# A fused attention and two-MLP kernel: another written order for its attention steps, and another split of the softmax sums

## The chip, the core and the metric

The kernel runs on one core of one Trainium2 chip. The metric is device time in microseconds (us), from start to end of one execution; a kernel's time is the median of three runs. The engines are TensorE (PE; its loads of weights are listed apart, as PEld), VectorE (DVE), ScalarE (ACT), GpSimd (POOL) and the queue that issues the transfers, SyncE (SP). Each engine works off its own list of instructions in order and waits on semaphores for what others have to deliver.

## What is computed

Attention in which two neighbouring queries are averaged first, and then two MLPs, all in 32-bit floats:

```python
# q, k, v: (2, 8, 1152, 64); q and k are scaled by 8 after the draw
q_pool = q.reshape(B, H, S // 2, 2, D).mean(axis=3)
scores = np.matmul(q_pool, k.transpose(0, 1, 3, 2)) / np.sqrt(D)
scores = scores - np.max(scores, axis=-1, keepdims=True)
attn = np.exp(scores)
attn = attn / (np.sum(attn, axis=-1, keepdims=True) + 1e-09)
x = np.matmul(attn, v)            # -> 1152 tokens x 512
h = x @ w_in                      # 512 x 2048
x = (h * np.tanh(softplus(h))) @ w_out          # 2048 x 512
h = x @ w_in2
out = np.where(h > 0, h, np.exp(np.minimum(h, 0)) - 1) @ w_out2
```

The MLP weights arrive as 64-bit floats and are turned into 32-bit floats on the chip, from their two 32-bit words.

## The kernel before

The program has two parts, `attention()` and then `mlps()`, and it orders everything itself: no scheduler moves an instruction.

**Attention** goes over eight pairs of heads (pairs 0 to 7, two heads side by side in the 128 partitions). A pair has 576 averaged queries, cut into a front part of 256 (c = 0) and a back part of 320 (c = 1), and nine tiles of 128 keys. The steps of a pair, with the two letters that the written order uses for them and the line that shows in the profile:

- LK, LQ, LV load keys, queries and values. PQ (L245) adds the two queries of a couple, HQ/DQ (L250, L253) and HK/DK/DF/HD (L265, L268, L274, L282, L278) split queries and keys into a high part and a small remainder for TensorE. In pair 0 the same steps come in pieces: XP, XH, XL, XK, XM.
- PM (L308, L315, L322, L325) multiplies high parts only, to find a bound of each row's largest score; PK (L332 to L337) reduces these products on VectorE; TP (L346, L349) takes the maximum over the pieces, TO and TI carry it through DRAM into a row `top` (in pair 0 FL and FC turn it on TensorE and ScalarE, L356 and L363).
- QK (L406, and L413 for the row `top`) makes the scores of one key tile (in the front part of two tiles at once), three products for the accuracy of 32 bits. EX (L424) takes the exponential into `pt`, which exists once for each part.
- AV (L498) multiplies the nine tiles of `pt` with the values.
- The sum over the keys, the divisor of the softmax, is made in SU (L452): TensorE multiplies with a matrix of ones and so adds over the 128 partitions. What it is fed is set by the table `SUMS`, one word of nine digits for each pair and part: a tile with 0 is multiplied directly; the tiles with 1 are first added to one another in a chain, AD (L436), on VectorE or GpSimd as the step's last digit says (1 or 0); the neighbouring tiles with 2 are added by one VectorE instruction, the gather GA (L441). So a word like 111111111 costs TensorE one product (four instructions of 32 columns of ones, which the profile lists as eight) and eight adds elsewhere; every 0 costs one more product, a chain that runs along with 2s gives two.
- SP, SO, SI, IN (L477), IO, II bring the sums through DRAM to their reciprocals and spread them; EV (L510) empties the AV product from its bank; SC (L515) scales it; TH and TL (L518, L522) split the result into XH and XL, the input of the MLPs.
- W steps prepare the first four weight slices of the MLP (WR loads, WB, WC on GpSimd, L126; WS, WW on VectorE, L131, L136, L137; WH, WL, L149).

All of PM, QK, AV and FL share four pairs of PSUM banks; the digit behind the tile number is the pair of banks. TensorE cannot begin a step before the reader of the former one on these banks (PK, EX, EV with SP) is through, and it does nothing else in the meantime.

The sequence of all these steps is the written list `ORDER`, 927 steps that the loop at the end of `attention()` calls one after the other; each step appends its instructions to the lists of its engines. `REST` holds steps of pair 7 that are put into the first units of the MLPs.

**The MLPs** go over 96 units (48 a layer) of 384 tokens by 128 hidden columns, the products L182 and L727. They are written by a loop of their own.

## Time and profile before

| | us |
|---|---|
| median of three runs (616.83 to 618.44) | 617.96 |
| the profiled execution's own time | 617.06 |
| its span, first to last instruction | 615.3 |
| TensorE busy | 595.5 (97%) |
| VectorE busy | 468.3 (76%) |
| ScalarE busy | 346.0 (56%) |
| GpSimd busy | 200.6 (33%) |

The span ends some 2 us short of the execution's own time. A matmul counts as busy from its issue to its modelled end, so a row of matmuls that come slowly still looks busy. The attention steps fill the first 213.19 us; there the engines lie much closer together than in these sums.

### The profile page before, as it was taken

Reading aid. Unit: us, or ns where it says so; the run is one execution under the profiler, and the core shown is the slowest. Engines: PE = TensorE matmul, PEld = TensorE weight load, DVE = VectorE, ACT = ScalarE, POOL = GpSimd, SP = SyncE. Lnnn points to the kernel's source line nnn. Section 1 sums busy time; section 2 is a strip of 40 time slices with the busy share of each in tenths; the row PEclk is TensorE's granted clock in tenths of the full one; section 3 lists DMA queues with packets and bytes.
Section 4 is the critical chain, followed back from the end, with each engine's and each line's share of the span. In section 5 each row is a group of like instructions: output and inputs, shape, how many; then the busy total and the mean of one; then the engine's idle time right before and its main releaser. Section 6 shows DMA issues by size and latency. Waiting matters only on the chain.

```text
span 615.3 us, 12110 instructions
## 1 busy us (share of the span) xinstructions
PE 595.5 (97%) x4856; PEld 517.7 (84%) x4856; DVE 468.3 (76%) x704; ACT 346.0 (56%) x666; POOL 200.6 (33%) x190
## 2 busy tenths in 40 slices
PE   5799999999999999999999999999999999999997
PEld 4576676676676699999999999999999999999996
DVE  6999999898995676754756667669878788995453
ACT  3677577675665555443454453466657667664442
POOL 5859567695482511111132323232110101100000
PEclk9989999999999999999999999999999999999999
DMA  8434255242221024322214222222132223300011
GB/s 281 147 97 143 64 156 162 54 128 76 74 50 22 13 80 148 118 64 92 94 45 137 69 69 80 92 70 73 66 102 70 68 69 107 122 13 17 36 52 51
DMA packets 46962, 53.39 MB, mean 87 GB/s; under 512 B 13818, under 2 KB 36410, under 8 KB 46906
## 3 DMA queue, kind: packets, MB, share of 16 engines
q1 hardware_dynamic: 46618, 52.22, 27.4%
q8 instruction: 38, 0.62, 0.5%
q10 hardware_dynamic: 288, 0.39, 0.2%
q14 instruction: 18, 0.15, 0.1%
HBM read 50.14 MB, written 2.47 MB: 85 GB/s over the span
## 4 chain that ended last, share of the span: by engine, by line
PE 82%; DVE 10%; DMA 2%; issue 2%; ACT 2%; POOL 1%; SPq 0%; POOLq 0%; DVEq 0%
PE banks L182 33%; PE banks L727 32%; PE banks L498 8%; PE banks L406 5%; DVE stat L332 4%; ACT pt L424 1%; PE banks L308 1%; PE banks L452 1%; DVE add L436 1%; POOL add L436 1%; DVE wf L137 1%; DMA top<-hopm 1%; DMA kr<-in_k_dram 1%; DMA tot<-hop 1%; PE banks L413 1%
## 5 line engine op out<-in xcount | busy, mean ns | idle before, releaser
L182 PE MATMUL banks<-XH,wl 128*128 128x384 f32 x384 | 128.4, 334 | 0.0
L182 PE MATMUL banks<-XL,wh 128*128 128x384 f32 x384 | 128.4, 334 | 0.0
L182 PE MATMUL banks<-XH,wh 128*128 128x384 f32 x384 | 128.3, 334 | 0.0
L126 POOL TENSOR_SCALAR wf<-wf 128x512 f32<-128x512 f32 x64 | 42.9, 671 | 257.1 <-ACT wf L122 226.9
L424 ACT ACTIVATE pt<-banks 128x640 f32<-128x640 f32 (+2 forms) x112 | 84.1, 790 | 23.5 <-PE banks L406 15.2
L332 DVE TENSOR_REDUCE stat<-banks 128x2 f32<-128x1024 f32 (+1 forms) x68 | 76.4, 1168 | 4.0 <-PE banks L308 3.5
L498 PE MATMUL banks<-pt,vr 128*32 128x320 f32 (+1 forms) x1152 | 73.2, 407 | 0.7 <-DVE stat L334 0.5
L182 PEld LDWEIGHTS banks<-XH,wh 128*128 128x128 f32 x384 | 72.1, 188 | 2.0 <-issue 0.3
L182 PEld LDWEIGHTS banks<-XL,wh 128*128 128x128 f32 x384 | 72.1, 188 | 1.6
L182 PEld LDWEIGHTS banks<-XH,wl 128*128 128x128 f32 x384 | 72.1, 188 | 0.0
L679 ACT ACTIVATE gh<-banks 128x384 fp32r<-128x384 f32 x48 | 23.7, 493 | 72.0 <-PE banks L182 72.0
L727 PE MATMUL banks<-gh,wh 128*128 128x384 f32 x192 | 64.1, 334 | 0.0
L727 PE MATMUL banks<-gl,wh 128*128 128x384 f32 x192 | 64.1, 334 | 0.0
L727 PE MATMUL banks<-gh,wl 128*128 128x384 f32 x192 | 64.1, 334 | 0.0
L498 PEld LDWEIGHTS banks<-pt,vr 128*32 128x32 f32 x1152 | 35.8, 110 | 33.3 <-ACT pt L424 1.9
L436 POOL TENSOR_TENSOR add<-add,pt 128x512 f32<-128x512 f32 (+1 forms) x35 | 51.6, 1475 | 27.2 <-DVE add L436 10.5
L727 PE MATMUL banks<-wl,gh 128*128 128x512 f32 x144 | 56.3, 391 | 0.0
L727 PE MATMUL banks<-wh,gl 128*128 128x512 f32 x144 | 56.2, 390 | 0.0
L727 PE MATMUL banks<-wh,gh 128*128 128x512 f32 x144 | 56.1, 390 | 0.0
L682 DVE TENSOR_TENSOR gl<-g,gh 128x384 fp32r<-128x384 f32 x48 | 32.5, 676 | 30.7 <-ACT g L680 30.6
L706 ACT CAST gh<-g 128x384 fp32r<-128x384 f32 x48 | 24.7, 515 | 48.1 <-DVE g L700 47.8
L137 DVE SCALAR_TENSOR_TENSOR wf<-raw,wf 128x512 int32<-128x512 int32 x64 | 48.0, 751 | 2.2
(101 smaller groups left out, 1219.7 us busy)
## 6 DMA issues: line engine op xcount, KB each, us to landing
raw<-in_moe_w_in_dram SPq DMA_DIRECT2D x28, 512.0 KB
raw<-in_moe_w_out_dram SPq DMA_DIRECT2D x28, 512.0 KB
vr<-in_v_dram SPq DMA_DIRECT2D x16, 288.0 KB
qr<-in_q_dram SPq DMA_DIRECT2D x14, 288.0 KB
kr<-in_k_dram SPq DMA_DIRECT2D x7, 384.0 KB
out_dram<-part SPq DMA_DIRECT2D x9, 256.0 KB
raw<-in_moe_w_in_dram SPq DMA_DIRECT2D x8, 256.0 KB
raw<-in_moe_w_out_dram SPq DMA_DIRECT2D x8, 256.0 KB
```

The costliest lines, as they stand in the source:

```text
L126: eng.tensor_scalar(self.f, self.f, HUGE, -HUGE, op0=ALU.min, op1=ALU.max)
L137: nc.vector.scalar_tensor_tensor(f, self.low, 29, f, op0=ALU.logical_shift_right, op1=ALU.bitwise_or)
L182: nc.tensor.matmul(pt[:, :TB], w[:, kk * P:(kk + 1) * P], x[:, kk, tk], start=(i == 0), stop=(i == len(terms) - 1))
L332: nc.vector.tensor_reduce(m[:, t, :, j], pt[:, :, :kw], axis=AX.X, op=ALU.max)
L406: nc.tensor.matmul(pt[:, h, t * w:(t + 1) * w], x[half[h], k0 + t * P:k0 + (t + 1) * P], y[half[h], cols], start=(z == t == 0 and not on), ...
L424: nc.scalar.activation(pts[n, c][:, kt:kt + m], pt, AF.Exp, scale=SCALE)
L436: eng.tensor_tensor(d, p[:, ch[0]] if len(ch) == 2 else d, p[:, k], op=ALU.add)
L498: nc.tensor.matmul(acc[n, c][32 * g:32 * (g + 1), 0, :w], vs[n][:, h, kt, 32 * z:32 * (z + 1)], pts[n, c][:, kt, h, :], start=(kt == 0), s ...
L679: nc.scalar.activation(gh, h, AF.Mish)
L682: nc.vector.tensor_tensor(gl, g, gh, op=ALU.subtract)
L706: nc.scalar.copy(gh, g)
L727: nc.tensor.matmul(pt, l, r, start=(first and i == 0), stop=(final and i == 2))
```

## The change

The list `ORDER` is written anew (920 steps), and so are `SUMS` and `REST`. Every step is the same code as before. No function changes. The word of digits of a pair's part, before and now (pair 0 to 7, front and back):

```diff
             SUMS = """
-            110122010 101111122 011111220 000022101 221111110 000111221 221111111 100111111
-            222111101 011111111 101111100 111111111 221111110 111111111 111111111 111111111
+            000002220 101101222 100001222 001011101 111110101 111100222 221111111 111102211
+            110111110 111110222 110111110 111101222 111101111 111111222 111111111 111111111
             """.split()
             ORDER = """
-            LV00 XP01 LV01 XK0 XH0 WR00 PM003 XM00 WR01 XK1 WR10 XP11 PM012 XM10 XK2 PK00 WR11 XH1 LV11 PM040 PK01
+            LV00 XP01 WR00 XK0 XH0 WR01 PM002 LV10 XK1 LV11 PK00 XP10 PM010 WR10 XM00 XH1 XK2 WR11 PM023 PK01 XL00
...
             REST = [
-                "SP70 SP71 SO70 SO71 SI70",
-                "SI71 IN70 IO70",
-                "IN71 IO71 II70",
-                "II71 SC70 TH70 TL70",
-                "SC71 TH71 TL71",
+                "IO70 EV71 SP71 II70",
+                "SO71",
+                "SI71 SC70 TH70",
+                "IN71 IO71 II71",
+                "SC71 TL70 TH71 TL71",
             ]
```

Counted over the attention: 48 products of sums become 52. The adds on VectorE go from 39 to 26, those on GpSimd from 47 to 50. The nine gathers stay nine: of two tiles of the front part 5 become 1, of three tiles of the front part 1 becomes 2, of two tiles of the back part 3 become none, of three tiles of the back part none become 6. Some splits and poolings change their engine.

Three places show how instructions move. The first is the list of TensorE around the front part of pair 0: the AV products (L498), the sums' products (L452; `pt` is a direct tile, `add` a chain or a gather), and the first peak products of pair 1. Before:

```order
L308 MATMUL banks<-KH,QH 128x384 x2
L325 MATMUL banks<-KH,blk_88 128x384 x3
L498 MATMUL banks<-pt,vr 32x256 x36
L452 MATMUL banks<-pt,ones 32x128 x12
L452 MATMUL banks<-add,ones 32x128 x8
L308 MATMUL banks<-KH,QH 128x512 x6
```

And now:

```order
L325 MATMUL banks<-KH,blk_88 128x384 x3
L406 MATMUL banks<-QH,KH 128x256 x2
L406 MATMUL banks<-QH,KL 128x256 x2
L406 MATMUL banks<-QL,KH 128x256 x2
L413 MATMUL banks<-top_84,unit 128x256 x2
L308 MATMUL banks<-KH,QH 128x384 x6
L498 MATMUL banks<-pt,vr 32x256 x36
L452 MATMUL banks<-pt,ones 32x128 x24
L452 MATMUL banks<-add,ones 32x128 x4
L308 MATMUL banks<-KH,QH 128x512 x6
```

Six tiles go directly into the product instead of three, the chain is gone and one gather is left; the other peak products of pair 0 now stand together ahead of AV.

The second is VectorE's list at the first peaks of pair 1 (L332 of 512 columns, L334, L336), with the weight steps (L131, L136, L137) and the first reciprocal (L477). Before:

```order
L441 TENSOR_REDUCE add<-pt 128x512
L131 TENSOR_SCALAR wf<-wf 128x512
L136 SCALAR_TENSOR_TENSOR wf<-raw,wf 128x512
L137 SCALAR_TENSOR_TENSOR wf<-raw,wf 128x512
L332 TENSOR_REDUCE stat<-banks 128x2 x2
L334 TENSOR_REDUCE stat<-banks 128x2x4
L332 TENSOR_REDUCE stat<-banks 128x2
L477 RECIPROCAL tot<-tot 128x4
L332 TENSOR_REDUCE stat<-banks 128x2
L346 TENSOR_REDUCE neg<-stat 128x2x2
```

And now, with the gather (L441) further up, ahead of two peaks and the maximum of pair 0:

```order
L441 TENSOR_REDUCE add<-pt 128x512
L332 TENSOR_REDUCE stat<-banks 128x2 x2
L346 TENSOR_REDUCE pad<-stat 128x4
L349 TENSOR_REDUCE pad<-stat 128x2
L131 TENSOR_SCALAR wf<-wf 128x512
L136 SCALAR_TENSOR_TENSOR wf<-raw,wf 128x512
L137 SCALAR_TENSOR_TENSOR wf<-raw,wf 128x512
L332 TENSOR_REDUCE stat<-banks 128x2 x3
L334 TENSOR_REDUCE stat<-banks 128x2x4
L336 TENSOR_REDUCE stat<-banks 128x2
L337 TENSOR_REDUCE stat<-banks 128x1
L332 TENSOR_REDUCE stat<-banks 128x2
```

The reciprocal, which stood between two peaks, now comes five rows behind these, after the maximum of pair 1 and another weight.

The third is VectorE's list between the back AV product of pair 5 and the front one of pair 6. Before:

```order
L274 TENSOR_TENSOR dr<-kr 128x896
L268 TENSOR_TENSOR KL<-kr,KH 128x256
L477 RECIPROCAL tot<-tot 128x4
L436 TENSOR_TENSOR add<-add,pt 128x640
L441 TENSOR_REDUCE add<-pt 128x512
L522 TENSOR_TENSOR XL<-out,XH 128x320
L332 TENSOR_REDUCE stat<-banks 128x2 x7
L436 TENSOR_TENSOR add<-add,pt 128x640
L334 TENSOR_REDUCE stat<-banks 128x2x4
```

And now:

```order
L274 TENSOR_TENSOR dr<-kr 128x896
L441 TENSOR_REDUCE add<-pt 128x640
L515 TENSOR_TENSOR out<-out,rb 128x320
L522 TENSOR_TENSOR XL<-out,XH 128x320
L477 RECIPROCAL tot<-tot 128x4
L332 TENSOR_REDUCE stat<-banks 128x2 x7
L477 RECIPROCAL tot<-tot 128x5
L334 TENSOR_REDUCE stat<-banks 128x2x4
```

The two adds of the back part are gone from here; a gather of three tiles of pair 5's back part takes the place of a gather of two tiles of pair 6's front part.

## Rows read from the trace of the kernel before

**Rows 1.** Busy time by stretch: us, then busy (count) of each engine, clock, DMA

```profile
0.00:69.45 69.45, 56.90 (x668) 41.66 (x668) 61.75 (x72) 41.56 (x76) 48.59 (x51) 0.95 0.49 153
69.45:166.86 97.41, 94.78 (x1375) 65.31 (x1373) 89.40 (x117) 65.04 (x109) 64.87 (x46) 1.00 0.38 109
166.86:182.25 15.39, 14.98 (x195) 10.64 (x193) 15.34 (x20) 12.03 (x19) 10.57 (x7) 1.00 0.25 49
182.25:213.19 30.94, 30.51 (x466) 19.49 (x466) 20.54 (x34) 15.40 (x27) 12.13 (x8) 1.00 0.09 18
213.19:615.30 402.11, 398.31 (x2164) 380.63 (x2160) 281.28 (x464) 212.01 (x440) 64.42 (x80) 1.00 0.24 77
```

**Rows 2.** TensorE in order of time (start, length): AV, sums' products, first MLP product

```profile
69.45 5.05 PE L498 MATMUL banks<-pt,vr 128*32 128x320 f32 x72
74.32 1.54 PE L452 MATMUL banks<-pt,ones 128*32 128x160 f32 x40
...
166.86 5.05 PE L498 MATMUL banks<-pt,vr 128*32 128x320 f32 x72
...
182.25 4.09 PE L498 MATMUL banks<-pt,vr 128*32 128x256 f32 x72
...
213.19 0.44 PE L182 MATMUL banks<-XH,wh 128*128 128x384 f32 x1
```

**Rows 3.** VectorE in the attention by line and form: busy, mean ns, idle before

```profile
L436 DVE TENSOR_TENSOR add<-add,pt 128x640 f32<-128x640 f32 x25 | 25.1, 1005 | 4.6 <-POOL add L436 4.2 <-ACT pt L424 0.2
L436 DVE TENSOR_TENSOR add<-add,pt 128x512 f32<-128x512 f32 x10 | 8.0, 803 | 3.2 <-ACT pt L424 3.1
L441 DVE TENSOR_REDUCE add<-pt 128x512 f32<-128x1024 f32 x5 | 6.2, 1245 | 0.0
L282 DVE TENSOR_TENSOR KL<-dr,DH 128x896 fp32r<-128x896 f32 x4 | 4.7, 1186 | 0.2 <-ACT DH L278 0.2
L441 DVE TENSOR_REDUCE add<-pt 128x640 f32<-128x1280 f32 x3 | 4.5, 1515 | 0.0
L441 DVE TENSOR_REDUCE add<-pt 128x512 f32<-128x1536 f32 x1 | 1.9, 1918 | 0.0
L274 DVE TENSOR_TENSOR dr<-kr 128x896 f32<-128x896 f32 x1 | 1.1, 1084 | 0.0
L253 DVE TENSOR_TENSOR QL<-qr,QH 128x576 fp32r<-128x576 f32 x1 | 0.8, 752 | 0.0
```

**Rows 4.** VectorE in order of time: instructions that waited or were held up

```profile
5.11 1.00 DVE L245 TENSOR_TENSOR qr<-qr 128x128 f32<-128x128 f32 x1 [1.02 <-DMA qr<-in_q_dram]
...
25.80 2.47 DVE L137 SCALAR_TENSOR_TENSOR wf<-raw,wf 128x512 int32<-128x512 int32 x1
...
33.59 0.18 DVE L477 RECIPROCAL tot<-tot 128x4 f32<-128x4 f32 x1 [0.79 <-DMA tot<-hop]
...
42.58 2.74 DVE L436 TENSOR_TENSOR add<-add,pt 128x640 f32<-128x640 f32 x1
...
172.66 8.01 DVE L332 TENSOR_REDUCE stat<-banks 128x2 f32<-128x1024 f32 x7
```

**Rows 5.** GpSimd in order of time, at two of these

```profile
25.18 2.55 POOL L282 TENSOR_TENSOR KL<-dr,DH 128x896 fp32r<-128x896 f32 x1
...
42.33 2.31 POOL L274 TENSOR_TENSOR dr<-kr 128x896 f32<-128x896 f32 x1
```

**Rows 6.** GpSimd by line and form

```profile
L436 POOL TENSOR_TENSOR add<-add,pt 128x512 f32<-128x512 f32 x22 | 29.9, 1358 | 11.8 <-DVE tot L477 6.8 <-DVE add L436 2.4 <-ACT pt L424 1.7
L436 POOL TENSOR_TENSOR add<-add,pt 128x640 f32<-128x640 f32 x13 | 21.7, 1673 | 15.4 <-DVE add L436 8.1 <-DVE neg L346 4.4 <-ACT pt L424 2.8
L274 POOL TENSOR_TENSOR dr<-kr 128x896 f32<-128x896 f32 x6 | 12.9, 2150 | 0.0
```

**Rows 7.** Busy time in two short stretches (columns as in the first group)

```profile
28.00:32.00 4.00, 1.76 (x11) 1.12 (x12) 4.00 (x5) 1.28 (x2) 3.21 (x3) 0.76 0.64 166
32.00:36.00 4.00, 4.00 (x21) 3.57 (x23) 3.18 (x6) 0.94 (x4) 1.12 (x2) 0.50 0.43 137
```

More of the change, by code (lines that the diff above doesn't have):

```diff
@@ new lines, in attention @@
+            PK18 QK0120 PQ20 EX012 PK13 QK0152 QK0113 EX015 TP10 WS2 QK0170 TO10 EX011 WW2 QK0141 EX017 QK0162 EX014
+            IN00 QK0183 AD0150 AD0121 EX016 TI10 PM190 QK0131 EX018 IO00 PK19 QK0102 WR40 EX013 PM163 EX010 PM171
+            AD0130 PK16 QK1000 HK21 HQ2 II00 PK17 HK20 PM152 AD0100 AV01309 EX100 PK15 DK200 TP11 GA01 DF20 TO11 WR50
+            WR51 TI11 SC00 TH00 SU01 WH2 TL00 LV20 EV01 WL21 LV21 PM251 SP01 HD2 QK1020 SO01 PK25 LK30 PM232 BQ2 PM213
+            DK210 LK31 EX102 PK23 WR41 QK1101 WB3 QK1040 PK21 EX110 PM222 WC3 EX104 QK1121 DQ20 PK22 QK1113 EX112
@@ new lines, in attention @@
+            II40 PM650 EX508 QK5143 TP60 PK65 QK5111 AD5040 TO60 EX514 LK70 PM692 EX511 QK5163 PK69 AD5050 PM670 EX516
+            QK5131 PK67 EX513 PM662 QK5183 AD5070 TI60 QK5151 IN41 SC40 AV50009 IO41 AD5060 TH40 EX518 TL40 EX515
+            AD5101 AD5120 PK66 II41 AD5151 AD5110 SU50 EV50 PM6830 SP50 SO50 QK5171 PK68 AD5130 QK6002 HK70 SI50 HQ7
+            TP61 AV51007 DF71 TO61 DK700 EX517 HK71 GA51 HD7 TI61 DQ70 SC41 AV51079 TH41 EX600 TL41 IN50 SU51 IO50
+            EV51 AD6000 AD6010 PM713 SP51 QK6022 PK71 II50 PM731 QK6100 EX602 PK73 PM773 LV71 EX610 QK6042 AD6030 LV70
```

89 lines of the change are left out of this document (39 added, 50 removed).

## The prediction

> **What bounds the kernel now.** I read the busy time by stretch first, because the sums over the whole span hide where a schedule matters. In the last stretch, the MLPs, TensorE is busy 398.31 of 402.11 us [rows 1]; no step of the attention list stands there but the hand-over of pair 7. That part is 65% of the span and I take it as fixed. Of the attention I marked the places at which TensorE begins a certain AV product [rows 2]: back part of pair 1 at 69.45, back part of pair 5 at 166.86, front part of pair 6 at 182.25, first MLP product at 213.19. VectorE is busy 61.75 of 69.45 us in the first stretch, 89.40 of 97.41 in the second, 15.34 of 15.39 in the third and only 20.54 of 30.94 in the fourth [rows 1]. ScalarE (41.56, 65.04) and GpSimd (48.59, 64.87) have room. So up to 182 us VectorE is the tightest engine, with TensorE close behind: TensorE starts a product when VectorE has freed its banks. From 182.25 on TensorE runs by itself, 30.51 of 30.94.
>
> The other thing to see is what VectorE loses to GpSimd. The weight step at 25.80 took 2.47 us and the add at 42.58 took 2.74 [rows 4], where adds of that form have a mean of 1.005 [rows 3]. In both cases a GpSimd instruction of 896 columns was under way (from 25.18 for 2.55 us, from 42.33 for 2.31 [rows 5]), and VectorE's ended some 0.5 us after it. Peaks do not show this: seven in a row took 8.01 us, 1.14 each [rows 4].
>
> **The change, by stretch.** I counted the instructions of each engine in the two lists up to the same AV products and priced the difference with mean durations. Two prices are not in the trace. A gather of three tiles of the back part (1920 columns a row): at least the 1.515 us of the two-tile one; at most 1.918 + 384 columns at the rate of the front part's step from two tiles to three, (1.918 - 1.245) / 512 per column = 0.50, so 2.42 [rows 3]. I take 2.35, since the 1.918 row is the nearest in size. Poolings, weight remainders and query remainders that go from GpSimd to VectorE: 0.75 each by the one row of such a width, 0.752 [rows 3]; the smallest of them is bounded by zero and that.
>
> *First stretch.* On VectorE go one add (0.80) and one key remainder (1.19), two gathers of each two-tile form (2 x 1.245 + 2 x 1.515 = 5.52) and the second pooling of pair 0; there come two three-tile gathers of the front (3.84), one of the back (2.35) and three moved steps (2.25). Without the pooling that is +0.93 us. The pooling was an instruction of 1.00 us that first waited 1.02 for its queries, ahead of all peaks [rows 4]; on GpSimd the first peak need not wait for it: -1.0. VectorE's work to the mark is therefore as before, -0.1. What can change is how it is interrupted. The first reciprocal waited 0.79 us for its transfer with peaks behind it [rows 4]; now two more peak steps, a maximum and three weight instructions stand ahead of it, more than 2 us: -0.8. GpSimd loses five adds of the front part, 5 x 1.358 = 6.8 us of its 48.59 [rows 6, 1], and gets more room between long instructions. The two hold-ups above cost (2.47 - 0.75) + (2.74 - 1.00) = 3.5 us; the long GpSimd instructions that caused them stay, so I count a quarter, -0.9. Against it: the gather of pair 0 stands ahead of the maximum that pair 0's back part waits for, 1.918 us where nothing stood: +0.8, taking less than half because a shorter run of peaks precedes it. TensorE gets five more products of sums; five took 1.54 us [rows 2]. They are free while VectorE is late and cost 1.5 where it is not; I count +0.4. Sum of the stretch: -0.1 - 0.8 - 0.9 + 0.8 + 0.4 = -0.6; and one thing that this leaves out, the clock, is a rival below. Bounds: -4.5 (all of the hold-ups and waits gone) to +2.3 (nothing gone, both costs whole).
>
> *Second stretch.* VectorE loses eight adds of the back part (8.04), one key remainder (1.19) and a gather of each front form (3.16); it gets two long gathers (4.70), one key difference (1.08), one query remainder (0.75), three moved steps (2.25) and a maximum of about 0.2: -3.4 us of 89.40. TensorE has three products fewer, 3 x 0.31 = -0.9. GpSimd gets four front adds and two back adds (4 x 1.358 + 2 x 1.673 = 8.8 [rows 6]); a key difference and a key remainder of one size change places; four steps of a row of GpSimd's length or so, 1.36 to 1.67 each, leave it: about +2.8 of 64.87, which fits into its idle third. VectorE is idle for 8 us of this stretch, so it does not set every step of it, and TensorE, at 94.78 busy of 97.41 [rows 1] with its matmuls spread out, cannot follow all the way. I take three quarters of VectorE's saving: -2.5. Bounds: -3.6 to +2.
>
> *Third and fourth.* To 182.25 VectorE loses two back adds (2.01), a small remainder and a front gather (1.245) and gets one long gather (2.35) and a reciprocal: -1.2. But the seven peaks that set this stretch (8.01 us) stay, they start when TensorE is through with pair 5's sums, and these have two products more, +0.62, ahead of the first peak. I take +0.2; bounds -0.8 to +0.8. From 182.25 on TensorE is the bound: one product fewer of pair 6's front part, one more of its back part, and pair 7's two unchanged: 0. Pair 7's adds lie mostly on VectorE, which is idle for 10 us here; its last chain ends ahead of the back AV's end as before. If it did not, TensorE's first MLP product would wait, up to one add, 1.0 us. The transfers of sums, maxima and weights move in SyncE's list with the steps they belong to; of pair 7 the front part's go out earlier and the back part's in later MLP units, needed only by the second and third token block: 0.
>
> Sum: -0.6 - 2.5 + 0.2 = -2.9 us. The profiled execution took 617.06 us (span 615.3), 0.9 below the median 617.96; from the one the sum gives 614.2, from the other 615.1. I forecast between the two, **614.7**.
>
> **Rivals.** *Nothing gained (617.1).* What VectorE saves in the second stretch is waited off, because TensorE, with matmuls from end to end, was as late as VectorE. For it: 94.78 of 97.41. Against it: a busy mark there includes waiting in the pipe, and VectorE's 92% is real work. Then only -0.6 + 0.2 stay: 616.7 to 617.6.
>
> *Slower (620.5).* The two-input instructions of VectorE meet GpSimd's long ones more often, in the second stretch. GpSimd works 2.8 us more there and VectorE's adds are in other places, so the distances that now keep them apart are new. One meeting with an 896-column instruction costs 1.74 us (2.74 against 1.00). Two more of them and the first stretch's hold-ups unchanged: -0.6 + 0.9 + 0.2 + 2 x 1.74 - 1.0 (what is left of the saving) = +3.0, so 620.1 to 621. It decides from two meetings more than before. The Trainium skill, SBUF — State Buffer, section "Who interferes with whom", says that a VectorE instruction with two SBUF inputs and a GpSimd instruction that reads SBUF lock each other out for a whole instruction, and that a reduce is never locked out. By that the gathers in the adds' place cannot be held up, but the added GpSimd work can be and can hold; the trace agrees as far as the 2.74 and the 1.14 per peak go.
>
> *Much faster (611.8).* Between 28 and 32 us TensorE was busy 1.76 of 4 us, waiting for peaks, and then the granted clock fell: 0.50 from 32 to 36, the 1.2 GHz level, with TensorE busy all of the 4.00 [rows 7]. If the first peaks of pair 1 come without the 2.47 us hold-up, TensorE stays busy and the clock at 2.4 GHz; the work of those 4 us then takes 2, and with the hold-up gone as well (1.7) some 3.7 us come on top of the sum's -2.9, less the 0.9 counted: -5.7. Against it: the weight step and the GpSimd remainder still stand near one another in both lists.
>
> **How the numbers follow.** The forecast's case (617.96 less 1.5 to 4.5) has 0.38, nothing gained 0.27, much faster 0.17, slower 0.18. A measurement of this kernel can tell about 0.3%, 1.85 us, from no change: below 616.1 is faster, above 619.8 slower. Of the forecast's case 0.36 lies below, 0.02 within; of the slower rival 0.17 above and 0.01 within. So faster 0.17 + 0.36 = 0.53, same 0.27 + 0.02 + 0.01 = 0.30, slower 0.17. For 8 in 10 the range leaves out a third of the much faster case and most of the slower one: 611.0 to 619.6.
>
> **What would show it.** Of the new profile: VectorE's busy time before the back AV of pair 5 lower by about 3 us and that AV at some 163.8 instead of 166.86; the first peak ahead of the 6.1 us (5.11 + 1.00) of now; no wait ahead of the first reciprocal; seven peaks of pair 7 still in about 8 us; from the front AV of pair 6 to the first MLP product 30.9 us again; MLPs 402 us. The forecast is wrong if that AV begins no earlier though VectorE did less (TensorE was the bound), if VectorE's adds have means above 1.1 us (meetings), or if the granted clock stays up through the first 40 us and the first mark comes 4 us sooner.

## The result

The changed kernel takes 610.29 us (median of five runs, 609.51 to 613.34) beside 616.83 for the kernel before in the same series: ratio 0.9897, 95% interval 0.9868 to 0.9927. The forecast was 614.7, range 611.0 to 619.6: the direction is right, the gain is twice what was forecast, and the median lies below the range. The profiled execution took 610.25 us with a span of 608.50.

The rows of after that answer [rows 1], in the same stretches (cut at the same AV products; us, then busy and count of PE, PEld, DVE, ACT, POOL, clock, DMA):

```profile
0.00:63.34 63.34, 54.48 (x708) 39.52 (x708) 54.56 (x71) 41.47 (x76) 39.57 (x45) 1.00 0.57 167
63.34:159.47 96.13, 93.77 (x1351) 64.92 (x1349) 86.84 (x117) 64.50 (x108) 66.16 (x48) 1.00 0.41 111
159.47:175.42 15.95, 15.44 (x210) 11.00 (x209) 13.72 (x15) 11.63 (x19) 11.07 (x10) 1.00 0.21 47
175.42:206.38 30.96, 30.54 (x466) 19.58 (x466) 22.44 (x33) 15.41 (x27) 14.44 (x9) 1.00 0.10 18
206.38:608.50 402.12, 398.31 (x2164) 380.62 (x2160) 280.97 (x463) 212.09 (x439) 64.84 (x80) 1.00 0.23 77
```

The first stretch is 6.11 us shorter (forecast 0.6), the second 1.28 (forecast 2.5), the third 0.56 longer (forecast 0.2), the fourth and the MLPs are as they were. So the surprise lies in the first 63 us. There VectorE is busy 7.2 us less (54.56 against 61.75), for work that I had counted as equal to within 0.1 us. The difference is made by VectorE instructions that were held up in before. Besides the three that [rows 4] shows (the pooling at 5.11, the weight step at 25.80, the add at 42.58), these four took 1.11, 1.11, 1.28 and 1.66 us:

```profile
23.52 1.11 DVE L131 TENSOR_SCALAR wf<-wf 128x512 int32<-128x512 int32 x1
24.66 1.11 DVE L136 SCALAR_TENSOR_TENSOR wf<-raw,wf 128x512 int32<-128x512 int32 x1
...
41.38 1.28 DVE L515 TENSOR_TENSOR out<-out,rb 128x256 f32<-128x256 f32 x1
...
57.27 1.66 DVE L137 SCALAR_TENSOR_TENSOR wf<-raw,wf 128x512 int32<-128x512 int32 x1
```

In after the same forms take 0.29 (pooling), 0.42 (L131), 0.69 (L136 and L137), 0.41 (L515) and 0.8 (the add). The seven together were some 7.4 us too long, which is about the whole fall of the busy time.

The same stretch by its AV products on TensorE, before and then after (start, length, operation; `[...]` is idle time and what ended it). Front and back part of pair 0, front part of pair 1:

```profile
20.84 4.09 PE L498 MATMUL banks<-pt,vr 128*32 128x256 f32 x72
43.82 5.05 PE L498 MATMUL banks<-pt,vr 128*32 128x320 f32 x72
60.12 4.09 PE L498 MATMUL banks<-pt,vr 128*32 128x256 f32 x72 [0.48 <-DVE stat L334]
```

```profile
18.80 4.09 PE L498 MATMUL banks<-pt,vr 128*32 128x256 f32 x72
38.02 5.05 PE L498 MATMUL banks<-pt,vr 128*32 128x320 f32 x72
53.41 4.09 PE L498 MATMUL banks<-pt,vr 128*32 128x256 f32 x72
```

2.0 us are there at the first, 5.8 at the second, 6.7 at the third; what comes behind adds nothing in sum. Most of it is thus made between 20 and 44 us. The first 2.0 go with ScalarE's copy of the front part's row of maxima (L363), which comes 1.6 us sooner, and with the first exponential behind it, at 13.54 instead of 15.43. Before, then after:

```profile
14.16 0.37 ACT L363 CAST top<-banks 128x256 fp32r<-128x256 f32 x1 [2.60 <-PE banks L356]
```

```profile
12.56 0.37 ACT L363 CAST top<-banks 128x256 fp32r<-128x256 f32 x1 [1.17 <-PE banks L356]
```

No run below puts that step alone back, so what brings these 2.0 us is not shown. Behind them, two things are different. The first is VectorE; these are its rows in after that answer [rows 4]:

```profile
23.02 0.54 DVE L131 TENSOR_SCALAR wf<-wf 128x512 int32<-128x512 int32 x1
23.60 0.69 DVE L136 SCALAR_TENSOR_TENSOR wf<-raw,wf 128x512 int32<-128x512 int32 x1
24.32 0.69 DVE L137 SCALAR_TENSOR_TENSOR wf<-raw,wf 128x512 int32<-128x512 int32 x1
25.01 3.49 DVE L332 TENSOR_REDUCE stat<-banks 128x2 f32<-128x1024 f32 x3
...
34.00 0.17 DVE L477 RECIPROCAL tot<-tot 128x4 f32<-128x4 f32 x1
...
40.08 0.17 DVE L346 TENSOR_REDUCE neg<-stat 128x4 fp32r<-128x12 f32 x1
...
40.22 2.35 DVE L441 TENSOR_REDUCE add<-pt 128x640 f32<-128x1920 f32 x1
```

The weight step of 2.47 us is one of 0.69, the reciprocal waits for nothing, and no add stands between the last peaks and the maximum at 40.08 (in before it began at 47.35). The second is the turn of pair 0's row of maxima (FL and FC, L356 on TensorE and L363 on ScalarE), without which no exponential of pair 0's back part (L424, 128x640) can begin. ScalarE before, then after:

```profile
33.41 0.37 ACT L363 CAST top<-banks 128x256 fp32r<-128x256 f32 x1 [1.95 <-PE banks L356]
33.68 0.43 ACT L367 CAST top<-banks 64x64 fp32r<-64x64 f32 x2
35.74 0.70 ACT L424 ACTIVATE pt<-banks 128x640 f32<-128x640 f32 x1 [1.64 <-PE banks L413]
```

```profile
28.40 0.37 ACT L363 CAST top<-banks 128x256 fp32r<-128x256 f32 x1 [0.15 <-PE banks L356]
28.66 0.42 ACT L367 CAST top<-banks 64x64 fp32r<-64x64 f32 x2
30.58 0.70 ACT L424 ACTIVATE pt<-banks 128x640 f32<-128x640 f32 x1 [1.49 <-PE banks L413]
31.91 5.05 ACT L424 ACTIVATE pt<-banks 128x640 f32<-128x640 f32 x8 [0.63 <-PE banks L413]
```

The first exponential comes 5.2 us sooner, which is nearly the 5.8 of the AV product that needs all nine. In before the turn stood behind two peak products that waited for VectorE (PM143 and PM130); after has it behind one (PM140). The third difference is the clock: it doesn't fall in the profiled execution of after (1.00 in the first stretch, 0.95 before); over the five executions its mean was 0.996 to 1.00, and the fastest, 609.51 us, had 0.997. So there were three candidates: VectorE's hold-ups and adds (theory A), the turn (theory H), the clock (theory C), and as a fourth the direct products by themselves (theory B). The first expectations below number A, B and C as theories 1, 2 and 3; a rival with a letter is a rival for that one kernel.

### The profile page after: what moved, and what is told of

The parts are those of the page before. It is cut to its first block, busy times and chain, and to the rows that moved or that the text cites. A ratio compares the mean times of both kernels' runs of the same rounds, so it can differ in the third digit from the quotient of the medians.

```text
span 608.5 us, 12165 instructions
## 1 busy us (share of the span) xinstructions
PE 592.5 (97%) x4888; PEld 515.6 (85%) x4888; DVE 458.5 (75%) x695; ACT 345.1 (57%) x666; POOL 196.1 (32%) x189
## 3 DMA queue, kind: packets, MB, share of 16 engines
HBM read 50.14 MB, written 2.47 MB: 86 GB/s over the span
## 4 chain that ended last, share of the span: by engine, by line
PE 85%; DVE 5%; ACT 5%; DMA 2%; issue 1%; SPq 1%; POOL 1%; DVEq 0%; POOLq 0%
PE banks L182 33%; PE banks L726 32%; PE banks L498 8%; PE banks L406 7%; ACT pt L424 4%; DVE stat L332 2%; PE banks L308 2%; DMA kr<-in_k_dram 1%; PE banks L452 1%; DVE add L441 1%; PE banks L413 1%; PE banks L322 0%; DMA hopm<-neg 0%; PE banks L315 0%; SPq L487 0%
## 5 line engine op out<-in xcount | busy, mean ns | idle before, releaser
L424 ACT ACTIVATE pt<-banks 128x640 f32<-128x640 f32 (+2 forms) x112 | 83.4, 790 | 21.8 <-PE banks L406 15.1
L332 DVE TENSOR_REDUCE stat<-banks 128x2 f32<-128x1024 f32 (+1 forms) x68 | 77.0, 1171 | 4.6 <-PE banks L308 3.7
L498 PE MATMUL banks<-pt,vr 128*32 128x320 f32 (+1 forms) x1152 | 73.1, 407 | 0.2
L436 POOL TENSOR_TENSOR add<-add,pt 128x512 f32<-128x512 f32 (+1 forms) x42 | 59.4, 1417 | 26.3 <-DVE add L436 9.7
L498 PEld LDWEIGHTS banks<-pt,vr 128*32 128x32 f32 x1152 | 35.9, 110 | 32.6 <-DVE stat L332 1.0
L705 ACT CAST gh<-g 128x384 fp32r<-128x384 f32 x48 | 24.7, 514 | 48.1 <-DVE g L699 47.8
L122 ACT ACTIVATE wf<-raw 128x512 f32<-128x512 f32 x64 | 43.2, 676 | 9.8 <-POOL wl L149 4.2
```

The lines of the kernel that those rows point to most:

```text
L122: nc.scalar.activation(self.f, self.top.bitcast(F32), AF.Identity, scale=2.0 ** -112)
L332: nc.vector.tensor_reduce(m[:, t, :, j], pt[:, :, :kw], axis=AX.X, op=ALU.max)
L424: nc.scalar.activation(pts[n, c][:, kt:kt + m], pt, AF.Exp, scale=SCALE)
L436: eng.tensor_tensor(d, p[:, ch[0]] if len(ch) == 2 else d, p[:, k], op=ALU.add)
L498: nc.tensor.matmul(acc[n, c][32 * g:32 * (g + 1), 0, :w], vs[n][:, h, kt, 32 * z:32 * (z + 1)], pts[n, c][:, kt, h, :], start=(kt == 0), s ...
L705: nc.scalar.copy(gh, g)
```

## Experiments: where in the list, and the clock

**The halves.** Before and after joined at the back AV product of pair 1, the words of `SUMS` with them (the digits of the banks are renamed where the lists meet):

```diff
 h_front: after's list up to AV11, before's list from there
 h_back:  before's list up to AV11, after's list from there
```

> The changed order and sums up to the back AV product of pair 1, the order and sums of before from there on (the numbers of the PSUM banks exchanged so that the two parts fit). The marks of the two traces put 6.1 of the 6.8 us won ahead of that product. If that is where the gain is made, this kernel is 5.5 to 6.5 us faster than before (616.8), so 610.5 to 611.5, and the product begins at 63.3 instead of 69.45. If the later part of the old order gives it back, because it was itself bound by something that does not move forward with the mark, it is 613 or more.

> The reverse: the order and sums of before up to the back AV product of pair 1, the changed ones from there on. By the marks it is 0.3 to 1.3 us faster than before, 615.5 to 616.5: the second stretch gives 1.3, the third takes 0.6. If the sums' new split in the later pairs carries the gain, as my forecast had it, it is 2.5 us faster or more, 614.3 or less.

Measured: h_front 612.36 us (ratio 0.9904, 0.9878 to 0.993), so after's first stretch brings nearly all (5.9 of 6.4 us by the ratios), though the time lies between the two that were expected. In its trace the clock did fall early, and the back AV of pair 0 came at 37.90 all the same (38.02 in after):

```profile
24.00:28.00 4.00, 2.70 (x19) 2.09 (x20) 3.84 (x5) 2.29 (x4) 4.00 (x3) 0.85 0.71 230
28.00:32.00 4.00, 3.99 (x30) 3.21 (x30) 3.63 (x5) 1.62 (x5) 2.84 (x3) 0.72 0.18 54
32.00:36.00 4.00, 4.00 (x58) 3.92 (x54) 3.66 (x7) 3.94 (x7) 0.00 (x0) 1.00 0.07 1
```

h_back took 624.12 us, but its renamed banks put pair 7's last AV product where the first MLP products go, and these overwrite it, so nothing past the attention is to be read from it. Its second stretch took 98.3 us: after's order there, and no gain on the 97.41 of before.

**The clock in before.** Eighteen unread products of 256 columns behind the last early peak product of pair 1, to keep TensorE busy where it waited [rows 7]:

```diff
-... PM100 PK12 ...
+... PM100 ZZ PK12 ...        (ZZ: 18 matmuls, result never read)
```

> Before with 18 products of 64x128 by 256 columns that nobody reads, put on TensorE where it waits for the first peaks of pair 1 (26.9 to 29.5 us); they end before that wait does. They add no wait and take none away; what they can do is to keep the clock at 2.4 GHz in 30 to 37 us. If the fall of the clock cost the time (theory 3), this kernel is 2 to 3 us faster than before, 614 to 615, with a granted clock of 1.0. If VectorE's hold-ups cost it, VectorE is as late as it was: within 0.7 us of before even with the clock at 1.0.

Measured: 617.87 us (ratio 0.9995, 0.9984 to 1.0006). The clock was low for 3.4 us instead of 6.8, and nothing came of it. A second, sharper experiment on the clock is below (a_fl_hot).

## Experiments: parts of the change alone, in before

```diff
 b_start (the second pooling of pair 0 on GpSimd)
-XP11
+XP10
 b_direct0 (pair 0's front chain taken out, its tiles go directly to the product)
-SUMS 110122010     AD0000 AD0011 AD0071 AD0030
+SUMS 000022000
 b_pool (GpSimd's key difference and key remainder of pair 1 elsewhere)
-... WC1 EX008 PK0b PM0c0 DF10 ...      ... WW1 DK110 SU00 ...
+... WC0 DF10 ...                       ... WL10 DK110 ...
 b_direct0_pool: both of the last two
 b_fl (the turn and one key tile's scores ahead of waiting peak products)
-PM100 PK12 .. PK10 .. PM143 .. PM130 .. PK13 FL13 WB2 .. PM1801 FC1 .. QK0153
+PM100 FL11 PK12 .. PK10 FC1 .. PM143 QK0151 .. PM130 .. PK13 WB2 EX015
 b_ws1 (weight steps behind four peaks; first reciprocal behind the maximum)
-GA00 WS1 WW1 .. PK12 PK10 PK14 PK13 IN00 PK11 TP10
+GA00 PK12 PK10 PK14 PK13 WS1 WW1 WH1 WL10 .. PK11 TP10 WS2 TO10 IN00
 b_add1 (two adds and a scaling behind the maximum of pair 1's back part)
-SC00 AD0161 AD0141 PK15 TP11 GA01 AD0130 TL00 DK211 SU01
+PK15 TP11 GA01 SC00 TL00 DK211 AD0161 AD0141 SU01   (AD0130 ahead of them)
 b_both: the last two together
```

> The order of before; only the second pooling of pair 0's queries goes from VectorE to GpSimd, so that the first peak on VectorE doesn't wait behind it (6.1 us before). Prediction's step: one us sooner at the first AV product (19.8) and at all marks after it, 616.8. Rival: the first peak waits for its products on TensorE anyway, or VectorE catches up by the first maximum (11.7), and nothing moves: 617.8.

> The order of before; only the chain of pair 0's front part is taken out (tiles 0, 1, 3 and 7 go directly into the product: seven direct tiles and the gather, 8 products of sums instead of 5; two VectorE adds of 0.75 us and one GpSimd add of 1.36 us fewer). Theory A (the gain of the first stretch is VectorE's hold-ups by GpSimd, and a new order alone moves them): some 1.5 us of adds go ahead of the first AV product, 20.8 to about 19.5, but the weight step of 2.47 us at the first peaks of pair 1 still meets a GpSimd remainder, so the back AV of pair 0 starts at 42 to 43 instead of 43.8 and the whole is 1 to 1.5 us shorter, 616.3 to 616.8. Theory B (the direct products are the gain by themselves): that AV at 40 or before and 613 to 614. Rival C (three more products cost TensorE their 0.3 us each, nothing else moves): 617.8 to 618.8.

> Before with two steps moved on GpSimd alone: pair 1's key difference goes ahead of the first weight remainder, and its key remainder (2.55 us at 25.18) behind the next weight remainder. Nothing changes in VectorE's list, in the sums or in TensorE's list. Theory 1, hold-ups: the three weight instructions of 23.5 to 28.3 us, held for 2.9 us in all, take 1.8 us together, the first peaks of pair 1 come 2 to 3 us sooner, TensorE does not starve, its clock stays at 2.4 GHz, and the back AV of pair 0 begins at 41 instead of 43.8: 613.5 to 615. Theory 2, the amount of work (direct products in place of adds): nothing of that is touched, within 0.5 us of before.

> As the kernel without pair 0's front chain, and GpSimd's key difference of 256 columns a half stands behind its second pairing of weight words and the second key remainder behind the weight remainder, as in the kernel that moved these two alone. There the moved difference held up the chain's add for 1.9 us; here that add is gone. Theory A: with no two-input work of VectorE beside either of them the first AV product comes at 19 to 20, the weight step takes 1.1 us instead of 2.5, and the back AV of pair 0 starts at 40 to 41 instead of 43.8: 614 to 615 in all. Theory B (direct products alone): no sooner than the kernel without the move. Rival D (the time is lost elsewhere before the end): marks 3 us sooner and 616.5 or more in all.

> The order of before; the turn of pair 0's row of maxima goes ahead of the peak products that wait for VectorE, and one key tile's scores and exponential with it, so that ScalarE has the first exponential of pair 0's back part some 4 us sooner. Theory H: that exponential at 30 to 32 instead of 35.7; one of nine is early, so the last is 0.7 to 1.5 us sooner, AV of pair 0's back part at 42.3 to 43 instead of 43.8, 616 to 617. If VectorE's hold-ups alone count: 617 to 618.

> The order of before; place 1 alone: the weight steps of VectorE that met a GpSimd key remainder at 25.8 (and the step of ScalarE that follows them) go behind the peaks of pair 1 that came after them, to where GpSimd waits for work, and the first reciprocal, which waited for its transfer there, goes behind the maximum of pair 1's front part. Theory A (the time of the first stretch lies in the hold-ups of VectorE's two-input steps ahead of peaks): the first peak of pair 1 starts at 24.5 to 25.5 instead of 28.2, that maximum (34.9 in before) ends by 32.5, the back AV of pair 0 starts at 41 to 42 instead of 43.8, and the whole takes 615 to 616. Theory B (VectorE's order there costs nothing, the direct products and the lower load make the gain): within 0.5 us of before. Theory C (the clock): it falls later or less, and the gain is there only if it doesn't fall at all.

> The order of before; place 2 alone: two adds of pair 0's back part on VectorE, of which one took 2.74 us beside a GpSimd key difference, and the scaling of pair 0's front part, go behind the maximum and the gather that the back AV of pair 0 and the row maxima of pair 1 wait for; GpSimd's last add of that chain comes before them. Theory A: the maximum of pair 1's back part ends at 43 to 44 instead of 47.6, and the AV product of pair 1's front part starts at 57 to 58 instead of 60.1: 614.5 to 616. It does not move the back AV of pair 0 (43.8). Theory B: within 0.5 us of before. Rival F (the adds meet the next GpSimd step or the sums' product waits for them): the maximum is early but the product of sums late, 616.5 to 618.

> Places 1 and 2 together, in the order of before. Theory A: the gains add, AV products at 41 to 42 (pair 0 back), 55 to 56 (pair 1 front), 64.5 to 65.5 (pair 1 back; before 69.4, after 63.3): 612.5 to 614, most of what the whole change brings. Theory B: within 1 us of before. Rival G (one place covers the other): no better than the better of the two alone.

| kernel | median us | ratio to before, 95% | back AV of pair 0 (43.8) | front AV of pair 1 (60.1) |
|---|---|---|---|---|
| b_start | 617.47 | 0.9998 (0.998 to 1.0015) | 44.0 | 60.0 |
| b_direct0 | 616.87 | 0.9981 (0.9967 to 0.9994) | 43.5 | 59.6 |
| b_pool | 620.99 | 1.0048 (1.003 to 1.0066) | 47.4 | 63.4 |
| b_direct0_pool | 620.69 | 1.0038 (1.0024 to 1.0052) | 46.9 | 62.9 |
| b_fl | 618.25 | 1.0009 (0.9993 to 1.0025) | 44.8 | 60.6 |
| b_ws1 | 622.81 | 1.0091 (1.0069 to 1.0113) | 51.2 | 66.9 |
| b_add1 | 622.57 | 1.0085 (1.0064 to 1.0107) | 44.3 | 65.1 |
| b_both | 627.15 | 1.0163 (1.0137 to 1.0189) | 49.6 | 70.1 |

The two marks are those of each kernel's one profiled execution. Only b_direct0 gains, 0.2%: theory B falls as far as pair 0's front part goes. Theory A's expectations missed in b_pool, b_direct0_pool, b_ws1, b_add1 and b_both. In the first four the trace shows why: the step that I moved took a place in a queue in which others stood behind it. In b_both the losses of b_ws1 and b_add1 nearly add up, to 10.2 us. One thing is mixed in: the first AV product, 4.09 us in before, ran partly at the low clock in b_pool (6.51 us), b_ws1 (5.66), b_direct0_pool (5.45) and b_add1 (5.26), and no run parts that from the order.

In b_direct0_pool the key difference waited for its keys on GpSimd, the weight remainder behind it was late, and ScalarE, which waited for that with its next weight step, had the last exponentials of pair 0's front part behind it. GpSimd, then ScalarE:

```profile
17.88 2.10 POOL L274 TENSOR_TENSOR dr<-kr 128x896 f32<-128x896 f32 x1 [5.00 <-DMA kr<-in_k_dram]
19.94 1.26 POOL L149 TENSOR_TENSOR wl<-wf,wh 128x512 fp32r<-128x512 f32 x1
```

```profile
21.23 0.66 ACT L122 ACTIVATE wf<-raw 128x512 f32<-128x512 f32 x1 [3.11 <-POOL wl L149]
21.79 1.50 ACT L424 ACTIVATE pt<-banks 128x1024 f32<-128x1024 f32 x2
```

In after the same key difference begins at 15.30; its keys' loads LK11 and LK10 stand ahead of LV01 in the list there, which I take for the reason. The move without the loads' new order costs 3 us at the next mark. The held add in b_pool (2.55 us instead of 0.70) came on top.

In b_ws1 the weight steps met no GpSimd instruction any more, and the first peak of pair 1 still began at 28.4 (28.19 in before): its products began on TensorE only at 27.86, behind an AV product that took 5.66 us at a low clock (from 21.0 for 3.4 us). In before they began at 25.95, and the peak waited for the held weight step; here the late TensorE took the step's place, so b_ws1 can't tell what the hold-up alone was worth in before. And ScalarE, which now had the rounding of the weights ahead of the turn, came to the turn at 37.40 instead of 33.41:

```profile
34.85 0.62 ACT L146 CAST wh<-wf 128x512 fp32r<-128x512 f32 x1 [6.56 <-DVE wf L137]
36.84 0.66 ACT L122 ACTIVATE wf<-raw 128x512 f32<-128x512 f32 x1 [1.37 <-POOL wl L149]
37.40 0.36 ACT L363 CAST top<-banks 128x256 fp32r<-128x256 f32 x1
...
39.61 0.70 ACT L424 ACTIVATE pt<-banks 128x640 f32<-128x640 f32 x1 [1.53 <-PE banks L413]
```

In b_add1 rival F came: the maximum was earlier (45.8 instead of 47.4), but the sums' product waited 4.19 us on TensorE for the adds, which now came behind a waiting key remainder, at 51.30, and took 2.49 us instead of 1.6:

```profile
53.84 0.75 PE L452 MATMUL banks<-add,ones 128*32 128x160 f32 x16 [4.19 <-DVE add L436]
```

In b_fl the turn on TensorE was early (28.2), but on ScalarE it stood behind the rounding of the weights, which waited for the held weight step, and one exponential of nine came at 32.7 and the next at 38.1. Nothing was gained.

## Experiments: parts undone, in after

```diff
 a_chain0 (pair 0's front chain put back)
-SUMS 000002220
+SUMS 110112220   and AD0000 AD0011 behind EX002, AD0030 behind DF10, AD0041 ahead of GA00
 a_add1 (two adds of pair 0's back part ahead of the last peak and the maximum)
-SUMS 101101222   PK17 .. PK15 DK200 TP11 GA01
+SUMS 101111122   PK17 .. AD0161 AD0141 PK15 DK200 TP11 GA01
 a_red1 (instead of these adds a reduce of about their work)
+PK17 .. ZR PK15 DK200 TP11 GA01    (ZR: tensor_reduce of tiles 6 and 7 into add[:, 1])
 a_fl (the turn behind three more peaks)
-PK11 WB2 FL11 FC1 PK14 PM1832 PM131 PK18 QK0120 EX012 PK13
+PK11 WB2 PK14 PM1832 PM131 PK18 PK13 FL11 FC1 QK0120 EX012
 a_fl_hot (a_fl, and 24 unread products of 128 columns in TensorE's three idle stretches there)
+PM113 Z(5) .. PM140 Z(9) .. PM131 Z(10)
 a_fl2 (the turn and the first key tile earlier than in after)
-PM113 .. SP00 .. PK10 PM140 PK11 WB2 FL11 FC1 .. QK0120 QK0152 QK0113 QK0170
+PM113 .. SP00 FL12 .. PK10 PM140 QK0121 PK11 FC1 WB2 EX012 .. QK0150 QK0112 QK0173
 a_tl (thirteen token remainders TL one VectorE step further back)
-SC00 TH00 .. TL00 LV20 EV01 WL21
+SC00 TH00 .. LV20 EV01 WL21 TL00
```

> The order of after; the chain of pair 0's front part is put back (tiles 0, 1, 3 and 4 added to one another, two adds on VectorE and one on GpSimd between the long key difference and the weight remainder; tiles 5 to 7 gathered as in after). Theory A: the first of these adds meets GpSimd's key difference (15.3 to 17.4) and is held until about 17.9, ahead of four peaks that the first AV product waits for: that AV at 20.5 to 21.5 instead of 18.8, and 2 to 3 us of the gain lost at all marks behind it, 612 to 613.5. Rival E (the adds cost their own work alone, and three products of sums fewer give some back): 0.5 to 1 us lost, 610.7 to 611.3. Rival C (fewer products help TensorE): at or under 610.3.

> The order of after, place 2 undone: two VectorE adds of pair 0's back part (tiles 6 and 4, as before) stand again ahead of the last peak and the maximum of pair 1's back part; the gather has two tiles instead of three. Theory A: the adds wait for GpSimd's add that ends at 39.7 and meet its key difference behind it, the maximum ends at 43 to 44 instead of 40.3, the AV product of pair 1's front part starts at 55.5 to 57 instead of 53.4: 612.5 to 614. Theory B (only their own 1.6 us less the shorter gather's 0.85): at most 1 us lost, 610.5 to 611.3.

> The order of after with one more reduce on VectorE (two tiles of pair 0's back part, 128x1280 to 128x640, the same as a two-tile gather; its result is overwritten by the gather behind it) in the very place where the kernel with two adds put back had them, ahead of the last peak of pair 1's back part. The two adds took 4.75 us there, 1.6 us of it their own work, 0.77 a wait for GpSimd's add and 2.4 a hold-up by GpSimd's key difference. Theory A (hold-ups and waits, not work): the reduce takes 1.5 us beside the same GpSimd instruction, the maximum of pair 1's back part ends at 41.5 to 42 instead of 40.3 (with the adds 45.3), the AV product of pair 1's front part starts at 54 to 55.2 (53.4; with the adds 57.7), 611 to 612. Theory B (any work there is paid several times over): as with the adds, 614 and more.

> The order of after; only the turn of pair 0's row of maxima for the back part (one step of TensorE, one of ScalarE) goes back behind three more peaks of pair 1, about where before had it. Theory H (the turn's place is a cause of its own): the first exponential of pair 0's back part starts at 34 to 35 instead of 30.6, the back AV product of pair 0 at 40.5 to 42 instead of 38.0, and 2 to 4 us of the gain are lost at every mark behind: 612.5 to 614. Theory A alone (only VectorE's hold-ups set the pace): the exponentials run late but VectorE, not they, sets the next peaks, and at most 1 us is lost.

> The kernel with the late turn (the turn of pair 0's row of maxima behind three more peaks), and 24 unread products of 128 columns on TensorE, in the stretches around 24.5, 26 and 30 us in which it waited for peaks there. Theory H (the order alone: the turn comes 4.1 us later): the clock stays up longer, but the back AV product of pair 0 is at 41.5 to 42.6 as without them (42.6), 615.5 to 616.5. Theory C (the low clock is the larger part of the loss): that AV at 40 or before, 612 to 613.5. In between, the difference is the clock's share; from the turn and the scores at either clock (9.6 against 8.4 us for the row of scores, 1.65 against 1.0 for the turn) I work out 1.9 us as the most that it can be, so 40.7 and 614.5.

> The order of after with the turn still earlier: into the banks that the sums' product of pair 0 leaves (25.9 instead of 27.4), and the scores of one key tile of pair 0's back part into the banks that it had, so that the first exponential starts at 28.3 to 28.8 instead of 30.6 and the eight others follow one place sooner. If the turn sets the pace: the back AV of pair 0 0.7 to 1.5 us sooner (36.5 to 37.3), 608.8 to 609.6. If VectorE's peaks set it from here on: 38.0 again and 610.3.

> The order of after; thirteen of the sixteen token remainders go one VectorE step further back, so that VectorE does that step while ScalarE rounds the scaled result (now it waits 0.47 to 0.53 us ahead of each of them, seven in the second stretch). If these waits are what the second stretch lacks to the forecast: up to 3.5 us less there, VectorE's wait gone, 607 to 609. If TensorE is as late as VectorE: 609.5 to 610.5. If the remainders meet GpSimd's adds in the new places: slower than after.

| kernel | median us | ratio to before, 95% | back AV of pair 0 (38.0) | front AV of pair 1 (53.4) |
|---|---|---|---|---|
| after | 610.29 | 0.9897 (0.9868 to 0.9927) | 38.0 | 53.4 |
| a_chain0 | 616.17 | 0.996 (0.9942 to 0.9979) | 41.1 | 56.6 |
| a_add1 | 615.89 | 0.9981 (0.9964 to 0.9998) | 38.2 | 57.7 |
| a_red1 | 612.31 | 0.9917 (0.9883 to 0.995) | 38.2 | 56.5 |
| a_fl | 616.4 | 0.9972 (0.9956 to 0.9988) | 42.6 | 58.0 |
| a_fl_hot | 616.62 | 0.998 (0.9966 to 0.9994) | 41.4 | 56.8 |
| a_fl2 | 610.55 | 0.988 (0.9856 to 0.9904) | 40.6 | 56.0 |
| a_tl | 610.99 | 0.9893 (0.9873 to 0.9912) | 38.5 | 53.9 |

By the intervals, a difference between two of these ratios is known to 2 or 3 us: the losses of a_chain0 (3.9), a_fl (4.6) and a_add1 (5.2) against after are clear of that, and so are the 3.9 us between a_add1 and a_red1; the 1.2 of a_red1 against after are not. The three clear losses are larger than theories A and H had set them.

**Adds against a reduce.** Two adds in one place and one reduce in the same place, first a_add1 (VectorE, and the GpSimd instruction beside them), then a_red1:

```profile
39.85 3.98 DVE L436 TENSOR_TENSOR add<-add,pt 128x640 f32<-128x640 f32 x2 [0.77 <-POOL add L436]
43.75 1.21 DVE L332 TENSOR_REDUCE stat<-banks 128x2 f32<-128x1024 f32 x1
45.00 0.17 DVE L346 TENSOR_REDUCE neg<-stat 128x4 fp32r<-128x12 f32 x1
...
40.46 2.68 POOL L274 TENSOR_TENSOR dr<-kr 128x896 f32<-128x896 f32 x1
```

```profile
38.95 1.52 DVE L459 TENSOR_REDUCE add<-pt 128x640 f32<-128x1280 f32 x1
40.38 1.22 DVE L332 TENSOR_REDUCE stat<-banks 128x2 f32<-128x1024 f32 x1
41.63 0.17 DVE L346 TENSOR_REDUCE neg<-stat 128x4 fp32r<-128x12 f32 x1
...
40.43 2.10 POOL L274 TENSOR_TENSOR dr<-kr 128x896 f32<-128x896 f32 x1
```

The maximum began at 40.08 in after, at 41.63 with the reduce, at 45.00 with the adds. The reduce costs its own 1.5 us; the adds cost 4.9, of which 1.6 is their work, 0.77 the wait for GpSimd's part of the chain and 2.4 the hold-up by a key difference (which grew itself, 2.68 against 2.10). That is theory A, shown with one place, one neighbour and two kinds of instruction. The AV product of the next part is 4.3 us later with the adds, and the whole 5.2 (0.9981 less 0.9897 of 617). With the reduce the whole is 1.2 us longer; its profiled run, 614.01 us and above its median, shows 3.1 us at that AV, with the clock low for 3.4 us from 28.3 and again from 48.8. In a_add1 it was low for 3.4 us from 47.0, so at the AV mark the hold-up can't be read by itself; at the maximum it can.

**The chain of pair 0.** Put back, its second VectorE add takes 1.76 us beside the weight remainder and the maximum behind it is 1.6 us late; the weight step behind that is held to 1.32 us. The back AV of pair 0 is 3.1 us late and the whole 3.9. Its clock was low for 6.8 us from 27.7, as long as in before, and what part of the 3.1 is the clock's isn't shown. The first AV product, which I had expected 2 us late, is not (18.5); the loss is made behind it. In before the same chain was worth 0.9 us (b_direct0).

**The turn and the clock.** a_fl adds no work at all, it only moves steps, and costs 4.6 us at the AV product and 4.6 in the whole (0.9972 less 0.9897). Here the clock was low for 10.2 us, after TensorE had been busy for 1.56 of the 4 us from 24. a_fl_hot takes that away: its granted clock is 1.00 through the whole execution. The same two stretches in a_fl, then in a_fl_hot:

```profile
28.00:32.00 4.00, 2.18 (x7) 1.25 (x7) 3.77 (x6) 0.00 (x0) 2.63 (x3) 0.50 0.12 40
32.00:36.00 4.00, 4.00 (x28) 3.78 (x29) 1.47 (x3) 1.70 (x5) 0.00 (x0) 0.50 0.09 5
```

```profile
28.00:32.00 4.00, 4.00 (x33) 3.52 (x32) 3.55 (x5) 0.29 (x1) 3.82 (x3) 1.00 0.38 107
32.00:36.00 4.00, 4.00 (x45) 3.64 (x44) 2.42 (x6) 1.98 (x6) 0.05 (x1) 1.00 0.03 1
```

The first exponential is at the same time in both, 34.62 and 34.70 (ScalarE of a_fl, then of a_fl_hot):

```profile
33.19 0.37 ACT L363 CAST top<-banks 128x256 fp32r<-128x256 f32 x1 [5.88 <-PE banks L356]
...
34.62 0.70 ACT L424 ACTIVATE pt<-banks 128x640 f32<-128x640 f32 x1 [0.72 <-PE banks L413]
```

```profile
34.70 5.64 ACT L424 ACTIVATE pt<-banks 128x640 f32<-128x640 f32 x9 [0.50 <-PE banks L413]
```

At the high clock the AV product is at 41.42, at the low one at 42.61: the clock's share at that mark is 1.2 of 4.6 us, the order's 3.4. But the profile of a_fl_hot was 0.73 us behind that of a_fl already at the first AV product (18.62 against 17.89), ahead of any filler. Counted from there the back AV comes 19.2 us later in after, 24.7 in a_fl and 22.8 in a_fl_hot: 1.9 of 5.5 for the clock, 3.6 for the order. The fillers left TensorE no idle time ahead of the turn, which by this count starts 0.4 us later than in a_fl, so up to 0.4 of the 3.6 may be theirs. In the whole nothing of it can be told (616.62 against 616.4); the second stretch took 99.4 us in a_fl_hot and 97.7 in a_fl. So theory H holds, and theory C explains a quarter to a third at one mark and nothing that can be told at the end.

**Earlier still.** a_fl2 gives 610.55, the ratio within the interval of after's: no gain that can be told. (In it the scores of one key tile of pair 0's back part are taken before the turned row is there: the kernel leaves out that tile's maxima, so its output is not the attention's and only its time can be read. That exponential waits for nothing, and even so the kernel isn't faster.) Its profiled run took 613.3 us, 2.7 above its median, with the clock low at the first AV product (5.78 us instead of 4.09); its marks say little.

**The second stretch.** In a_tl VectorE no longer waits ahead of most token remainders (2.0 us of L522's waits in the attention left of 6.5), and the time is the same, 610.99. In the second stretch 2.9 us of these waits went; VectorE's waits for peak products there grew from 2.1 to 5.1 us and those for GpSimd's adds from 0.7 to 1.7. VectorE alone isn't what sets the second stretch.

## Why the prediction was wrong, and where it was right

*First stretch, -0.6 forecast, -6.1 measured: this step failed.* Two of its terms were mis-sized and one was missing. The hold-ups I had counted as two meetings of 3.5 us together, of which a quarter goes, because the long GpSimd instructions stay. The stretch had seven hold-ups of some 7.4 us, and all went (four of them, 2.9 us, had no term at all; the pooling I had only as a step that moves away): in after none of VectorE's two-input steps up to 63 us is held by more than 0.2 us, and its busy time is 7.2 us lower. The bound of -4.5 for "all gone" was too small for the same reason. a_add1 and a_red1 show what such a meeting costs there: 2.4 us beyond the work, and 0.77 of waiting for the other engine's part of the chain. The adds of pair 0's chain I had priced as work alone; put back in after they cost 3.9. Missing was the turn: I read the list of TensorE between 26 and 38 us without asking what its rows waited for, and so had no term for FL and FC, whose place alone is worth 4.6 us in after. The terms that I did price were small, and came out partly: the reciprocal's wait went (-0.8); the first peak began 0.3 us sooner and not 1.0, since its products were not there (b_start shows no gain); the maximum of pair 0's back part, with the gather ahead of it, came 0.7 us later (+0.8 forecast).

The prices don't add up to 6.1: single undone parts cost 3.9, 4.6 and 5.2, and single parts done in before make it from 0.9 us shorter to 5.8 longer. The gain belongs to the parts together. As I read it, peaks on VectorE, turn and scores on TensorE, exponentials on ScalarE and the key splits on GpSimd form one loop here, and each part only takes away what would be late next; that reading is argued, and what brings the 2.0 us ahead of the first AV product stays open.

*Second stretch, -2.5 forecast, -1.3 measured.* VectorE's saving was there, 2.6 us (3.4 counted), and the sizes were right: the long gather, estimated at 2.35, has a mean of 2.358. (In the list of gathers ahead of the prediction one count is off: of two tiles of the back part one stays, and five, not six, have three tiles. The sums by stretch had them right.) But the share that I let through was too large. a_tl took away 4.5 us of VectorE's waits for ScalarE in the attention, and others grew in their place. Moreover the stretch isn't a fixed number: after's order of it took 96.1 us in after, 96.2 in a_add1, 97.5 in a_chain0, 98.3 in h_back, 99.4 in a_fl_hot, and before's order 97.4 in before and 98.8 in h_front. What precedes it shifts it by up to 3.3 us, so I don't call the 1.3 a gain of the order. Which steps meet in the longer ones I didn't follow up; that stays open.

*Third, fourth, MLPs.* Right: +0.56 (within its bounds), 0.02, 0.01. The seven peaks took 8.12 us. Of the signs that I had named against the forecast one came: the clock stayed up in the first 40 us and the first mark came 6.1 us sooner, where I had set 4. VectorE's busy time up to the back AV of pair 5 fell by 9.8 us, not 3, and that AV came at 159.47, not 163.8.

*The rivals.* "Nothing gained" and "slower" (more meetings in the second stretch) didn't come; the adds of the back part there have means of 0.82 and 0.93 us, not above 1.1. "Much faster, 611.8" came out nearest in size and the clock did stay up, but its mechanism isn't the cause: h_front has the gain with a low clock, b_dummy half the low clock and no gain, a_fl_hot the loss at a clock of 1.00.

The Trainium skill, SBUF — State Buffer, section "Who interferes with whom", was cited for the lock between a VectorE instruction with two SBUF inputs and a GpSimd instruction that reads SBUF, and for reduces being exempt. The pair of a_add1 (3.98 us for two adds of 0.8) and a_red1 (1.52 for the reduce) agrees in both halves. The gathers of after, 2.36 us each, stood beside GpSimd instructions without growing.

## What to carry to other kernels

Where four engines hand small tiles around in a ring, count more than the work on the tightest one: write down for each engine what stands ahead of the step that opens the next run of work (here a turned row of maxima), because a step that costs 1 us of TensorE was worth 4.6 by its place here. Two adds on VectorE beside a GpSimd instruction of 2.68 us were held up by 2.4, a reduce in the same place took only its own 1.52; put reduces or TensorE products ahead of the steps that others wait for, and chains behind them. When you price such hold-ups, list every instruction that is longer than its form takes undisturbed, not the two longest. And don't expect such a change to come apart: test its parts by undoing them in the new kernel, since done alone in the old one they meet the queues that the rest of the change has cleared.

## What the runs showed of the hardware

GpSimd suffers from a meeting as well: its key difference took 2.68 us beside the adds and 2.10 beside the reduce. VectorE's integer steps on weight words are held up too, those with one input among them: L131, 0.42 us undisturbed, took 1.11 in before at 23.52 and 1.32 in a_chain0, each beside a GpSimd instruction (L245 from 22.92 for 1.43 us, L253 from 24.23 for 1.41). A fall of TensorE's clock to its 1.2 GHz level (0.50), in the places read here after TensorE had waited, was cheaper than I thought: 10.2 us of it cost 1.2 to 1.9 us at the next mark (a_fl against a_fl_hot) and nothing that could be told by the end.
